# One order list of a fused attention and dense-layer kernel, rearranged; the last outputs finished one at a time

## The chip, the cores and the metric

The kernel runs on one core of a Trainium2 chip. The metric is the device time of one execution in microseconds; where several runs are shown, it is their median. The engines are called by the profile's names: PE multiplies matrices, DVE works on vectors, ACT applies functions, POOL does further element work, and SP issues most of the transfers.

## The reference

The input x has 2048 rows of 512 elements in bf16. It is normalized row by row (xn), and three terms are added: x itself, an attention with a compressed memory, and a dense layer with a gate function.

```python
xn = layernorm(x)
out = x + A(xn) + silu(xn @ w1) @ w2          # w1: 512 x 1792, w2: 1792 x 512

def A(xn):                                     # 32 heads of 16, 4 segments of 512 rows
    q, k, v = heads(xn @ wq), heads(xn @ wk), heads(xn @ wv)
    M, z = 0, 0
    for s in range(4):
        p = softmax(q[s] @ k[s].T * 0.25 + mask)            # each row sees itself and earlier ones
        a_mem = (phi(q[s]) @ M) / (phi(q[s]) @ z + 1e-6)    # phi(t) = t + 1 above 0, else exp(t)
        o[s] = g * a_mem + (1 - g) * p @ v[s]               # g = sigmoid(beta)
        M += phi(k[s]).T @ v[s];  z += sum(phi(k[s]))
    return o @ wo
```

## The kernel before

The work is cut into small pieces. Each piece is a word in one long string, `ORDER`, and the loop at the end of the kernel calls the pieces in exactly this order. Every engine gets its instructions in the order of the words and works through them in that order; what one engine needs of another is a wait. So the string fixes the queue of every engine, SP's transfers too. A word has a kind, then numbers: the segment s (0 to 3) first, then a block dt of 128 channels (8 heads), a row tile j of 128 rows or a block of w1's columns, then a part.

The score pieces `S0` to `S79` are the backbone. Each forms scores of eight heads' worth of queries and keys in the one four-bank PSUM tile psS, then issues the exponential on ACT (line 669) into one of seven buffers Pb, and the mask of the diagonal on POOL (line 677). Piece t belongs to segment t // 20, block (t // 5) % 4 and batch t % 5; batches 2, 3 and 4 also read kTo, a masked copy of the keys which POOL makes. In what follows a stage is what stands from one S to the next, numbered in the order of the list: stage 1 begins with S1. Each line of `ORDER` is one stage.

The other words:

- `k`, `q`, `v`, `h`: parts of the products of xn with wk, wq, wv, w1. `kv`, `qv`, `vv` copy a finished product out of PSUM on DVE, `ka`, `qa`, `va` on ACT; `kv` and `ka` also issue POOL's kTo. `ha` is the tanh on ACT and `hv` the product on DVE that makes hT.
- `E`, `O`: weighing, the product of Pb and v for even and odd heads (16 column-tiled matrix products, line 696). `Ev`, `Ov` copy the result on DVE, `Ea`, `Oa` on ACT; the even ones also issue two transfers on SP (the softmax sums to zraw), the odd ones six.
- `fp`, `fa`, `fv` and `gp`, `ga`, `gv`: phi of k and of q, on POOL, ACT and DVE. `t`: a transposing transfer of phi(k). `m`, `mv`, `mw`: the update of the memory.
- `s`, `sv`, `r`, `w`, and for the last segment `fill`, `R`, `W`: denominators and their reciprocals on DVE. `z`, `d`: two transfers each on SP that spread the reciprocals over the channels (spr). `zv`, `dv`: the products with them on DVE. `n`: the product phi(q) M, added to the attention output oT by `nv` on DVE.
- `o`, `oc`, `od`: one product of an output tile, whole, in halves or in quarters of its columns; products 0 to 13 read hT and w2, 14 to 17 read oT and wo. `oh` is the same for the very last tile (segment 3, row tile 3), which is done in two halves of 256 columns. `xl` loads 128 rows of x for the sum (x_res, line 579). `st` adds it and stores a whole tile of 128 x 512 (lines 586 and 591); `sh` does that for a half of the last tile (lines 633 and 637).
- `xs`, `xg`, `Nv`, `XD`, `X`, `Xv`, `Xa`: statistics, root, normalization and transposition of x. `X` transposes on PE, and `Xv` (DVE) or `Xa` (ACT) copies the result; `XD` is a transposing transfer. `lw` loads w2 and wo.

The tile psS takes four PSUM banks, and a pool of four more serves all other products; a piece that opens a product waits until the copy or addition that reads the bank's former content has ended. Tiles of x_res and of the normalized rows share four places in SBUF in the same way.

PE works in three tilings: rows (scores), columns (weighing, denominators) and whole. The k, q, v, h, m, n and o pieces can run whole (128 x 128) or as four column pieces of 32 (line 324); the loop picks, for the pieces after a score piece, the tiling of the next weighing piece or score piece that follows, so that few changes are needed.

Of the kernel before, what the change touches and what calls it, by code (L numbers as in the profile page):

```python
# [16 lines left out]
kind odd ones0 ones1 zeros xc0 xd0 xc1 xq0 xi0 Nv0 busy44 xd1 xq1 xc2 xi1 X0.1 Nv1 xd2 Xa0.1 busy6 v0.0.0 v0.0.1 xq2 X1.1 Xa1.1 xs3 v0.0.2 v0.0.3 xq3 v0.1.0 xi2 v0.1.1 v0.1.2 v0.1.3 Nv2 xi3 X2.1 va0.0 k0.2.0 va0.1 Nv3 Xv2.1 X3.1 Xv3.1 k0.0.0 k0.0.1 k0.0.2 k0.0.3 q0.0.0 kv0.0 tb q0.0.1 q0.0.2 xs4 q0.0.3 qa0.0 k0.2.1 q0.3.0 fa0.0 q0.1.0  # L17
S1 k0.2.2 xs6 q0.1.1 v0.3.0 v0.3.1 xs7 q0.3.1 q0.1.2 q0.1.3 xs5 xg4.4 q0.3.2 qa0.1 q0.3.3 fp0.0
S2 k0.2.3 v0.3.2 qv0.3 v0.3.3 k0.1.0 kv0.2 fp0.2 fa0.2 k0.1.1 vv0.3 k0.1.2 k0.1.3 q0.2.0 q0.2.1
S3 kv0.1 q0.2.2 h0.10.0 h0.10.1 Nv4 fv0.0 q0.2.3 h0.10.2 v0.2.0 h0.10.3 qv0.2 ha0.10 k0.3.0 k0.3.1  # L20
S0 Nv5 v0.2.1 k0.3.2 hv0.10 h0.11.0 k0.3.3 h0.11.1 h0.11.2 kv0.3 h0.11.3 Nv7 xs8 XD5 ha0.11 h0.7.0
S7 h0.7.1 h0.1.0 h0.7.2 h0.7.3 v0.2.2 h0.1.1 v0.2.3 XD4 h0.1.2 h0.1.3 hv0.11 Nv6 ha0.7
S6 h0.13.0 fp0.3 XD7 h0.13.1 vv0.2 hv0.7 E0 XD6 v1.1.0 h0.13.2 h0.13.3 ha0.1 v1.1.1 Ev0
S5 fv0.2 h0.5.0 v1.1.2 h0.5.1 hv0.1 v1.1.3 vv1.1 v1.3.0 h0.5.2 ha0.13 xs14 hv0.13 h0.5.3 ha0.5 t0.2 v1.3.1
S9 hv0.5 xs12 q1.1.0 v1.3.2 v1.3.3 fa0.3 q1.1.1 q1.1.2 E1 k1.1.0 q1.1.3
S4 qv1.1 k1.1.1 vv1.3 fv0.3 k1.0.0 k1.0.1 k1.0.2 lw0 h0.4.0 k1.1.2 Ev1 h0.4.1 k1.0.3 k1.1.3 kv1.1
S17 h0.8.0 h0.8.1 kv1.0 h0.4.2 O0 xs10 h0.4.3 h0.2.0 Ov0 ha0.4
S10 h0.2.1 k1.2.0 xs11 xs9 k1.2.1 h0.2.2 k1.2.2 h0.2.3 h0.8.2 ha0.2 t0.3 hv0.4 xg8.4 t0.0 k1.2.3
# [805 lines left out]
```

## Time and profile before

| | us |
|---|---|
| median of 3 runs | 228.55 (228.10 to 229.02) |
| the profiled execution | 229.09 |
| its span | 227.40 |
| PE, ACT, DVE, POOL busy | 217.2, 198.0, 177.7, 113.9 |
| S1 begins on PE | 12.27 |
| S78, the last score piece, begins | 206.18 |
| PE's last product ends | 223.60 |

The granted clock of PE is 1.00 throughout. The profile's times count from the start of the span. A line of the timeline has the start, the length, the engine with the line of the kernel, what is written from what, the number of instructions merged into it, and in square brackets how long the engine had been idle and what ended that. Lines with SPq are SP issuing transfers, not the transfers.

### The profile page before, as it was taken

To read this page: it belongs to the slowest core of one execution; us is meant where nothing else is said; L and a number is where in the kernel's file an instruction comes from. 1 tells how busy PE (TensorE), PEld (TensorE's weight loads), DVE (VectorE), ACT (ScalarE), POOL (GpSimd) and SP (SyncE) were. 2 spreads that over 40 slices of the span, in tenths; PEclk is the share of its full clock that TensorE was granted. 3 is DMA by queue.
4 is the path that set the end of the run, shared out by engine and by line. 5 is a ranking of instruction groups with operands and counts; after the bars stand their busy time and mean duration, and the time that the engine had idled before them with its cause. 6 is when DMAs were issued, how large, how long until landed. Compare 5 with 4: busy or idle time off the path is not lost.

```text
span 227.4 us, 7543 instructions
## 1 busy us (share of the span) xinstructions
PE 217.2 (96%) x3124; PEld 112.9 (50%) x3152; DVE 177.7 (78%) x351; ACT 198.0 (87%) x179; POOL 113.9 (50%) x173
## 2 busy tenths in 40 slices
PE   8999999999999999999999999999999999999993
PEld 8666645545534434444444434445444444445662
DVE  5799899987787897658798798747676888887834
ACT  3799998999999999999999899999999989897000
POOL 6059647667454673665644577546474265342000
PEclk9999999999999999999999999999999999999999
DMA  6992429323215213404314212141032212024122
GB/s 181 361 381 68 77 52 299 60 55 57 61 22 158 72 35 47 96 15 112 41 40 113 75 53 58 35 117 42 22 100 66 88 36 84 29 63 130 29 90 94
DMA packets 34787, 20.55 MB, mean 90 GB/s; under 512 B 15680, under 2 KB 34240, under 8 KB 34752
## 3 DMA queue, kind: packets, MB, share of 16 engines
q1 hardware_dynamic: 32128, 17.45, 28.3%
q10 hardware_dynamic: 2624, 2.62, 3.6%
q8 instruction: 24, 0.39, 0.8%
q14 instruction: 11, 0.09, 0.1%
HBM read 9.96 MB, written 2.10 MB: 53 GB/s over the span
## 4 chain that ended last, share of the span: by engine, by line
PE 62%; ACT 11%; DVE 11%; DMA 8%; issue 4%; SPq 2%; POOL 0%; DVEq 0%
PE ps L322 18%; PE psO L322 14%; PE psS L662 9%; ACT Pb L669 8%; PE ps L324 8%; PE psO L324 6%; PE psV L696 6%; DMA x_hi<-in_A_x_dram 4%; DMA spr<-rz 3%; ACT th L457 2%; DMA x_res<-in_A_x_dram 2%; DVE stats L272 1%; DVE o_out L586 1%; DVE kT L361 1%; PE psM L324 1%
## 5 line engine op out<-in xcount | busy, mean ns | idle before, releaser
L669 ACT ACTIVATE Pb<-psS 128x2048 bf16<-128x2048 f32 x80 | 150.2, 1878 | 5.8 <-PE psS L662 5.1
L677 POOL TENSOR_SCALAR_AFFINE_SELECT Pb<-Pb 128x512 bf16<-128x512 bf16 (+1 forms) x112 | 80.1, 729 | 85.1 <-ACT Pb L669 83.7
L462 DVE SCALAR_TENSOR_TENSOR hT<-th,ps 128x512 bf16<-128x512 bf16 x56 | 37.8, 679 | 14.1 <-ACT th L457 13.7
L322 PE MATMUL ps<-xnT,w_sb 128*128 128x512 bf16 (+1 forms) x177 | 43.3, 340 | 0.8 <-issue 0.5
L322 PE MATMUL psO<-w_sb,hT 128*128 128x512 bf16 (+2 forms) x139 | 36.1, 340 | 0.7 <-issue 0.5
L457 ACT ACTIVATE th<-ps 128x512 bf16<-128x512 f32 x56 | 32.8, 597 | 0.5 <-PE ps L322 0.4
L324 PE MATMUL psO<-w_sb,hT 128*32 128x128 bf16 (+2 forms) x468 | 26.7, 300 | 0.0
L322 PEld LDWEIGHTS <-w_sb 128*128 128x128 bf16 x184 | 17.1, 98 | 16.3 <-issue 3.3
L696 PE MATMUL psV<-Pb,Vz 128*32 128x128 bf16 (+3 forms) x512 | 23.1, 300 | 0.4 <-DVE oT L573 0.2
L322 PEld LDWEIGHTS <-hT 128*128 128x128 bf16 x149 | 13.6, 97 | 16.9 <-issue 4.8
L324 PE MATMUL ps<-xnT,w_sb 128*32 128x512 bf16 (+1 forms) x384 | 21.8, 329 | 0.0
L324 PEld LDWEIGHTS <-hT 128*32 128x32 bf16 x636 | 15.7, 97 | 9.7 <-issue 1.7
L696 PEld LDWEIGHTS <-Vz 128*32 128x32 bf16 x512 | 13.0, 96 | 10.6 <-issue 1.4
L662 PE MATMUL psS<-qT,kT 16*128 16x128 bf16 (+3 forms) x256 | 17.3, 301 | 0.9 <-ACT Pb L669 0.8
L662 PE MATMUL psS<-qT,kTo 32*128 32x384 bf16 (+3 forms) x256 | 17.2, 299 | 0.6 <-ACT Pb L669 0.2
L362 POOL TENSOR_SCALAR kTo<-kT,pm_odd 128x512 bf16<-128x512 bf16 x16 | 11.9, 747 | 8.2 <-DVE kT L361 7.3
L322 PE MATMUL ps<-xnT,wk_sb 128*128 128x512 bf16 (+1 forms) x66 | 15.4, 328 | 0.7 <-issue 0.5
L322 PE MATMUL ps<-wv_sb,xnT 128*128 128x512 bf16 x48 | 14.3, 380 | 0.6 <-issue 0.2
L662 PEld LDWEIGHTS <-kT 16*128 16x128 bf16 x256 | 5.9, 91 | 16.7 <-issue 16.2
L361 DVE CAST kT<-ps 128x512 bf16<-128x512 f32 x15 | 10.2, 687 | 4.6 <-PE ps L322 4.3
L586 DVE SCALAR_TENSOR_TENSOR o_out<-psO,x_res 128x512 bf16<-128x512 f32 x14 | 9.6, 687 | 5.3 <-PE psO L322 2.8
L719 DVE CAST oraw<-psV 128x512 bf16<-128x512 f32 x16 | 11.0, 688 | 3.4 <-PE psV L696 3.3
(105 smaller groups left out, 298.3 us busy)
## 6 DMA issues: line engine op xcount, KB each, us to landing
spr<-rz SPq DMA_DIRECT2D x56, 64.0 KB
x_res<-in_A_x_dram SPq DMA_DIRECT2D x16, 128.0 KB
out_dram<-o_out SPq DMA_DIRECT2D x15, 128.0 KB
w_sb<-in_B_w_dram SPq DMA_DIRECT2D x1, 1792.0 KB
w_sb<-in_B_w_dram ACTq DMA_DIRECT2D x1, 1792.0 KB
x_hi<-in_A_x_dram SPq DMA_DIRECT2D x2, 512.0 KB
oraw<-odd SPq DMA_DIRECT2D x64, 16.0 KB
wv_sb<-in_A_wv_dram SPq DMA_DIRECT2D x2, 256.0 KB
```

Of the source, the lines that this page charges most:

```text
L322: return [nc.tensor.matmul(out, lhsT=lhsT, rhs=rhs, start=start, stop=stop, skip_group_check=True)]
L324: nc.tensor.matmul(out[c : c + 32], lhsT=lhsT[:, c : c + 32], rhs=rhs, start=start, stop=stop, tile_position=(0, c), skip_group_check=True,)
L361: copy(out=kT[:, dt, :], in_=sts[s].pop(("k", dt))[:, :])
L362: nc.gpsimd.tensor_scalar(out=kTo[:, dt, :], in0=kT[:, dt, :], scalar1=pm_odd[:, 0:1], scalar2=1.0, op0=ALU.mult, op1=ALU.mult,)
L457: nc.scalar.activation(out=th[:], in_=sts[s]["h", ft][:, :], func=AF.Tanh, scale=0.5)
L462: nc.vector.scalar_tensor_tensor(out=st["hT"][:, ft, :], in0=st.pop(("th", ft))[:], scalar=1.0, in1=st.pop(("h", ft))[:, :], op0=ALU.add, ...
L586: out = nc.vector.scalar_tensor_tensor(out=o_out[:], in0=st.pop(("psO", j)), scalar=0.5, in1=st["x", j][:], op0=ALU.mult, op1=ALU.add)
L662: nc.tensor.matmul(psS[:, g, c0 : c0 + nq], lhsT=kk[rows, dt, kt * P : (kt + 1) * P], rhs=st["qT"][rows, dt, kt * P : L], start=True, stop ...
L669: exp = nc.scalar.activation(out=Pb[:, :, :], in_=psS[:, :, :], func=AF.Exp, scale=SCALE)
L677: mask = nc.gpsimd.affine_select(out=blocks, in_=blocks, compare_op=ALU.is_ge, fill=0.0, base=0, pattern=[[0, blocks.shape[1]], [1, P]], c ...
L696: nc.tensor.matmul(psV[32 * g : 32 * g + 32, kt * P : L], lhsT=Vzs[s % 2][:, kt, 4 * dt + g, par : par + 2, :].rearrange("p a d -> p (a d) ...
L719: copy(out=oraw[:], in_=sts[s].pop(("psV", 0))[:, :])
```

## The change

Only the string `ORDER` differs. It has 1324 words before and after, and all but six are the same words at other places. Six change the engine of a copy: `Xv2.1` becomes `Xa2.1`, `kv3.2` becomes `ka3.2` and `ka3.3` becomes `kv3.3`, `Ov14` becomes `Oa14`, `Ev15` becomes `Ea15`, and `Oa15` becomes `Ov15`. The order of the score pieces changes too, near where they stood (the first are S1 S2 S3 S0 S7 S6 S5 before and S1 S4 S2 S5 S0 S3 S7 after). The last outputs end in the order st3.0, sh0, st3.2, st3.1, sh1 before, and sh1, st3.2, st3.0, sh0, st3.1 after, with other products between them; two of the residual loads stand before them in the last stage, xl3.1 and xl3.0 before, xl3.1 and xl3.2 after.

The diff, cut to the stages that the prediction speaks of (each line one stage; the last is the whole last stage):

```diff
-kind odd ones0 ones1 zeros xc0 xd0 xc1 xq0 xi0 Nv0 busy44 xd1 xq1 xc2 xi1 X0.1 Nv1 xd2 Xa0.1 busy6 v0.0.0 v0.0.1 xq2 X1.1 Xa1.1 xs3 v0.0.2 v0.0.3 xq3 v0.1.0 xi2 v0.1.1 v0.1.2 v0.1.3 Nv2 xi3 X2.1 va0.0 k0.2.0 va0.1 Nv3 Xv2.1 X3.1 Xv3.1 k0.0.0 k0.0.1 k0.0.2 k0.0.3 q0.0.0 kv0.0 tb q0.0.1 q0.0.2 xs4 q0.0.3 qa0.0 k0.2.1 q0.3.0 fa0.0 q0.1.0
-S1 k0.2.2 xs6 q0.1.1 v0.3.0 v0.3.1 xs7 q0.3.1 q0.1.2 q0.1.3 xs5 xg4.4 q0.3.2 qa0.1 q0.3.3 fp0.0
...
-S3 kv0.1 q0.2.2 h0.10.0 h0.10.1 Nv4 fv0.0 q0.2.3 h0.10.2 v0.2.0 h0.10.3 qv0.2 ha0.10 k0.3.0 k0.3.1
...
-S7 h0.7.1 h0.1.0 h0.7.2 h0.7.3 v0.2.2 h0.1.1 v0.2.3 XD4 h0.1.2 h0.1.3 hv0.11 Nv6 ha0.7
...
-S5 fv0.2 h0.5.0 v1.1.2 h0.5.1 hv0.1 v1.1.3 vv1.1 v1.3.0 h0.5.2 ha0.13 xs14 hv0.13 h0.5.3 ha0.5 t0.2 v1.3.1
-S9 hv0.5 xs12 q1.1.0 v1.3.2 v1.3.3 fa0.3 q1.1.1 q1.1.2 E1 k1.1.0 q1.1.3
...
-S49 ga2.3 kv3.2 dv1.1 o1.0.13 k3.0.0 Ev9 Ov8 gv2.2 o1.2.1 k3.0.1 n1.2 kv3.0 o1.2.7 zv1.1 o1.0.11 nv1.2
-S51 o1.2.2 h2.0.0 o1.2.8 h2.0.1 gp2.0 o1.0.6 n1.1 ha2.0 o1.2.16
-S54 o1.2.11 mw1.0 zv1.3 o1.2.12 od1.2.5.3 nv1.1 z1.0 o1.2.6 o1.0.10 hv2.0 xl2.3 gp2.3 O9 oc1.2.10.1 oc1.0.9.0 Ov9 od1.2.5.2 n1.3 ga2.0
...
-S53 o1.0.17 od1.2.5.1 oc1.1.9.1 od1.1.7.2 gv2.3 o1.0.8 mw1.2 E10 o1.2.17 o1.2.14 o1.1.11 oc1.1.9.0 ga3.3 Ev10
...
-S78 o3.0.5 h3.11.0 o2.1.17 st2.1 h3.11.1 E15 o3.0.6 o3.2.1 oh1.1 o3.1.8 Ev15 ha3.11 oc3.0.3.1 oh0.1 O15 oh12.1 o3.2.3 o3.2.5 hv3.11 zv3.1 oh5.1 o3.2.8 n3.2 Oa15 oh13.0 o3.1.3 o3.1.12 dv3.1 zv3.2 nv3.2 o3.2.7 oc3.0.11.1 oc3.0.11.0 oh9.0 n3.0 oh16.0 n3.1 zv3.0 o3.2.9 o3.1.1 oc3.1.0.1 o3.1.13 o3.2.0 oc3.1.0.0 o3.2.12 o3.2.6 nv3.0 od3.1.11.2 nv3.1 oh11.1 o3.1.14 oh15.1 o3.2.11 oh0.0 R1.1 R1.0 oh10.0 o3.0.14 od3.0.10.2 oh8.0 od3.1.11.3 d3.3 oh15.0 od3.0.10.0 R1.3 o3.1.6 R1.2 oc3.1.9.0 oc3.1.9.1 o3.1.5 oh2.0 o3.1.10 W1 oh14.0 o3.2.13 oh1.0 o3.1.15 oh5.0 o3.0.15 o3.0.16 dv3.3 z3.3 od3.0.10.1 o3.2.15 xl3.1 o3.2.16 zv3.3 o3.2.2 n3.3 oh11.0 od3.1.11.1 oh3.1 oh10.1 oh6.0 oh4.1 nv3.3 o3.1.4 od3.0.10.3 oh4.0 oh12.0 o3.2.4 o3.0.13 oc3.0.3.0 oh3.0 o3.0.17 xl3.0 st3.0 o3.2.14 od3.1.11.0 oh7.0 o3.2.17 oh17.0 oh7.1 sh0 o3.2.10 o3.1.2 oh2.1 o3.1.7 o3.1.16 st3.2 o3.1.17 oh17.1 st3.1 oh6.1 oh13.1 oh14.1 oh16.1 oh8.1 oh9.1 sh1
+kind odd ones0 ones1 zeros xc0 xd0 xc1 xq0 xi0 Nv0 busy44 xd1 xq1 xc2 xi1 X0.1 Nv1 xd2 Xa0.1 busy6 v0.0.0 v0.0.1 xq2 X1.1 Xa1.1 xs3 v0.0.2 v0.0.3 xq3 va0.0 v0.1.0 v0.1.1 xi2 Nv2 xi3 v0.1.2 Nv3 v0.1.3 X2.1 va0.1 k0.0.0 X3.1 k0.0.1 k0.2.0 Xv3.1 k0.2.1 Xa2.1 k0.0.2 k0.0.3 q0.0.0 q0.0.1 q0.0.2 tb q0.0.3 q0.1.0 kv0.0 k0.2.2 xs5 qa0.0 q0.3.0 fa0.0
+S1 k0.2.3 k0.1.0 xs6 kv0.2 q0.1.1 xs4 q0.1.2 q0.1.3 xs7 k0.1.1 k0.1.2 qa0.1 q0.3.1 fp0.0 xg4.4 k0.1.3 kv0.1
...
+S3 XD6 XD7 v1.1.0 xs10 hv0.7 h0.5.2 h0.5.3 ha0.5 h0.1.3 xs12 v1.1.1 XD4 v1.1.2 v1.1.3 vv1.1 h0.13.0 h0.13.1 ha0.1 hv0.5
+S7 xl0.1 xs11 h0.13.2 h0.13.3 hv0.1 v1.3.0 v1.3.1 E0 ha0.13 v1.3.2 Ev0
...
+S50 o1.0.10 od1.2.5.0 n1.1 kv3.0 h2.0.0 h2.0.1 o1.2.9 nv1.1 o1.2.6 ha2.0 n1.3
+S51 oc1.2.0.0 nv1.3 hv2.0 t2.3 o1.2.16 o1.2.15 O9 o1.0.8 o1.1.8 Ov9 o1.2.4 zv1.0 o1.1.0
...
+S52 o1.2.11 ga3.3 o1.0.15 oc1.1.4.1 oc1.2.10.0 xl2.3 oc1.2.10.1 dv1.0 hv2.2 od1.2.5.3 od1.1.7.3 n1.0 od1.2.5.2 o1.2.17 oc1.2.0.1 od1.2.5.1 nv1.0 o1.1.3 o1.2.7
+S56 o1.0.14 o1.2.14 E10 gv2.3 o1.2.13 o1.2.2 oc1.1.9.0 fa2.2 o1.0.16 Ev10 o1.2.12
...
+S64 od1.3.12.0 r2.1 h2.9.1 hv2.10 r2.2 h3.1.0 w2 h3.1.1 d2.1 o2.3.0 gp3.2 z2.3 oc1.3.1.0 od1.3.12.1 o2.3.6 ha2.9 ha3.1 st1.3 hv2.9 o2.3.7
+S60 hv3.1 oc2.3.13.0 fill o2.3.3 h3.3.0 h3.3.1 m2.2 d2.3 h3.0.0 ha3.3 od2.3.9.0 mv2.2
...
+S66 h2.12.1 h3.4.0 h3.4.1 o2.0.1 ha2.12 od2.3.9.3 oc2.3.2.1 ha3.4 o2.0.8 o2.0.4
...
+S78 hv3.11 o3.1.12 dv3.1 o3.1.5 z3.0 o3.1.2 o2.1.15 z3.2 E15 o3.0.12 o3.0.8 o2.1.6 dv3.2 o3.2.12 oh11.1 o3.0.1 oh9.1 z3.1 oh1.1 Ea15 O15 oh7.1 o3.0.7 o3.1.1 Ov15 d3.3 oc3.1.9.1 o3.0.5 o3.2.0 n3.2 od3.0.10.3 oh2.0 od3.1.11.0 zv3.2 od3.0.10.2 zv3.0 od3.0.10.1 oh6.1 od3.1.11.1 oh13.1 o3.1.4 o3.1.13 nv3.2 oh10.1 od3.0.10.0 n3.0 od2.1.12.0 o3.2.9 oh5.1 o3.2.2 nv3.0 od3.1.11.3 R1.3 oh8.1 oc3.0.3.1 oh16.0 o3.2.14 R1.0 o3.1.14 o3.2.1 R1.1 oh14.0 oc3.0.3.0 o3.1.3 R1.2 oh4.1 W1 zv3.1 oh3.1 oc3.0.11.1 oh9.0 n3.1 oh7.0 z3.3 oh8.0 o3.0.14 oh5.0 o3.2.8 o3.2.6 oh13.0 xl3.1 oh10.0 st2.1 o3.2.4 o3.2.5 nv3.1 o3.2.3 o3.0.16 dv3.3 oc3.1.9.0 oh14.1 o3.2.16 o3.0.15 oh6.0 zv3.3 oh16.1 o3.2.13 oh15.1 o3.0.13 xl3.2 n3.3 nv3.3 o3.2.10 o3.2.15 o3.2.7 o3.2.11 oh2.1 od3.1.11.2 oh12.1 oh0.1 oh17.1 o3.0.17 oc3.0.11.0 o3.2.17 oh4.0 o3.1.15 oh0.0 o3.1.7 sh1 oh1.0 o3.1.10 st3.2 oh15.0 oc3.1.0.0 oh11.0 st3.0 oh12.0 oh3.0 oh17.0 o3.1.17 o3.1.16 sh0 o3.1.8 oc3.1.0.1 st3.1
```

## The prediction

> **What bounds the kernel now.** I read the page's busy shares first, then busy times by stretch, then the order of time around single stages and at the end. The change is one list of pieces in another order, so what counts is where an engine waits.
>
> ```profile
> PE 217.2 (96%) x3124; PEld 112.9 (50%) x3152; DVE 177.7 (78%) x351; ACT 198.0 (87%) x179; POOL 113.9 (50%) x173
> L669 ACT ACTIVATE Pb<-psS 128x2048 bf16<-128x2048 f32 x80 | 150.2, 1878 | 5.8 <-PE psS L662 5.1
> ...
> 12.27:36.86 24.59, 23.38 (x324) 14.77 (x328) 23.36 (x47) 23.58 (x21) 15.53 (x22) 1.00 0.51 153
> 36.86:61.00 24.14, 23.29 (x359) 12.60 (x363) 20.58 (x43) 24.06 (x22) 16.00 (x24) 1.00 0.38 89
> 206.18:223.60 17.42, 17.42 (x441) 11.04 (x440) 11.61 (x23) 2.95 (x3) 0.85 (x2) 1.00 0.25 74
> 223.60:227.40 3.80, 0.00 (x1) 0.00 (x0) 0.69 (x2) 0.00 (x0) 0.00 (x0) 1.00 0.36 116
> ```
>
> The last four rows are stretches of the span: length, then busy PE, PEld, DVE, ACT, POOL. PE and ACT are both full to the 80th score piece at 206.18, then PE alone is, to 223.6; 3.8 us follow without PE. In the first stretch (ten stages) DVE is 95% busy too.
>
> ```profile
> 65.82 0.39 PE L662 MATMUL psS<-qT,kTo 32*128 32x512 bf16 x4
> 66.27 1.88 ACT L669 ACTIVATE Pb<-psS 128x2048 bf16<-128x2048 f32 x1
> 68.20 0.39 PE L662 MATMUL psS<-qT,kT 16*128 16x512 bf16 x4
> 68.64 1.88 ACT L669 ACTIVATE Pb<-psS 128x2048 bf16<-128x2048 f32 x1 [0.50 <-PE psS L662]
> ```
>
> This is the ring that sets the pace: a score piece, 0.45 us later its exponential of 1.88, 0.05 later the next score piece, since the one psS tile must be free: 2.38 us from S to S. One tanh (0.60) on ACT takes the 0.50 that is idle here. On PE a 512-column product costs 0.216 start to start, a weighing piece 0.54, a score piece 0.335. A stage whose PE work sums to 2.28 also lasts 2.38, so each stage costs max(2.38, PE work + 0.105).
>
> **The part that is arithmetic.** Both lists have the same number of score, weighing and product pieces (202.06 us of PE work by these prices) and, as the code picks the tiling, 160 changes of tiling each. By the rule the 79 stages from S1 to S78 sum to 192.46 us before and 192.40 after (PE work in them 180.55 and 180.49; work a stage lacks to 2.28: 3.62 and 3.61): -0.06. Measured before: 206.18 - 12.27 = 193.91. So only 1.45 us are waits in the stages, and these the change can gain or lose.
>
> **The waits of before, and what becomes of them.**
>
> ```profile
> 22.25 0.10 PEld L662 LDWEIGHTS <-kTo 32*128 32x128 bf16 x4 [0.29 <-POOL kTo L362]
> 29.14 1.08 ACT L457 ACTIVATE th<-ps 128x512 bf16<-128x512 f32 x2
> 30.09 1.90 ACT L669 ACTIVATE Pb<-psS 128x2048 bf16<-128x2048 f32 x1
> 136.49 0.45 PEld L696 LDWEIGHTS <-Vz 128*32 128x32 bf16 x16 [0.72 <-DVE oT L573]
> ```
>
> Fifth stage (S7), 0.29: kT's copy kv0.1 comes two stages before its use. The new list has it in stage 1 and S7 in stage 7: -0.29.
>
> Eighth stage (S9), 0.25: two tanh pieces in one stage start the next exponential at 30.09, 0.35 later than 29.29 + 0.45. The new list has a pair in S3, and the next stage (S7) has only 1.96 us of PE work, so all 0.37 shows: +0.12. The pair of S16 (0.25 over two stages) has its twin in the new S15: 0. New pairs stand in S64 and S66; the next stages hold 2.44 and 2.55 us of PE work, which cover 0.16 and 0.27 of 0.37 each: +0.30. Before, the late pairs stood beside a stage of 2.93 us and cost nothing.
>
> Stage 52 (S54), 0.43: weighing piece O9 waits for a PSUM bank that nv1.1 frees late; DVE had 5.31 us of work put into stage 50 (two kv at 0.69, Ev, Ov and nv at 0.69, gv 0.83, zv 0.56, dv 0.47). The new list puts at most 2.6 us into any of stages 48 to 52, but O9 still follows the adder of its bank (nv1.3) by only 0.43 us of PE work. Bounds -0.43 and 0; I take -0.43, as DVE no longer runs late. Stage 55, 0.22: E10 waits for a mask. There S52's mask (1.1 us) now precedes E10 at 0.87 us of PE work: stays.
>
> **What the change adds early.** Stages 1 to 10 gain one more statistics pair (0.67 + 0.18) and one more hT (0.66) on DVE: 23.36 + 1.51 = 24.87 us for 24.59. What is late on DVE frees banks late, and the h and k products wait for these. Bounds: 0 (PE works on what it has) and +1.5 (all of it shows); I take the overload, +0.30, as DVE's 1.2 us of idle time there can be filled. In stages 11 to 20 DVE has 2.4 us less, so the debt ends there.
>
> **Head.** X2.1's copy moves from DVE (0.42) to ACT (a 512-wide copy there, 0.59, row of Vz), behind va0.1 which ends at 9.57: k0.0.2 may start at 10.2 for 10.08: S1 +0.07. The exponential's table load behind it ends at 11.6, before qa0.0's input.
>
> **The end.** Times from S78 = 0 (206.18).
>
> ```profile
> 218.06 0.43 SPq L579 DMA_DIRECT2D x_res<-in_A_x_dram  x1
> ...
> 221.75 0.69 DVE L586 SCALAR_TENSOR_TENSOR o_out<-psO,x_res 128x512 bf16<-128x512 f32 x1 [1.52 <-PE psS L324]
> 222.35 0.41 DVE L633 SCALAR_TENSOR_TENSOR o_half<-psS,x_res 128x256 bf16<-128x256 f32 x1
> ...
> 223.28 0.68 DVE L586 SCALAR_TENSOR_TENSOR o_out<-psO,x_res 128x512 bf16<-128x512 f32 x1
> ...
> 223.88 0.41 DVE L633 SCALAR_TENSOR_TENSOR o_half<-psS,x_res 128x256 bf16<-128x256 f32 x1
> 224.77 0.34 SPq L637 DMA_DIRECT2D out_dram<-o_half  x1
> ```
>
> Before, the first output addition starts when the load issued at 218.06 has landed (its bracket names PE, but the chain that ended last names this load, 3.60), and five additions run back to back: 0.60 after a whole one, 0.34 after a half one. DVE ends at 18.11, the last store goes out at 18.59, the span ends at 21.22.
>
> After, PE has 17.03 us of work for 17.19 and ends at 17.26. Counting products back, sh1 has its last product 1.73 before that, st3.2 1.40, st3.0 1.08, sh0 0.32, st3.1 at the end. sh1 can start at 15.73 (0.2 from product to reader), then DVE again sets the spacing: 16.07, 16.67, 17.27, 17.61, end 18.30: +0.19. So the outputs are spread in the list but not on DVE. The final store was issued 0.48 after DVE's end; the other four 0.03 to 0.15. I take 0.25: -0.23. The final store is 128 KB for 64 KB, which took 2.63 from issue to the span's end; a 128 KB load took 3.60. Bounds 0 and +0.97; +0.20, nearer the row that is a store. The end: +0.16.
>
> [...]
>
> SP's queue is in order: the list now puts xl3.2, one of the four residual loads, behind O15's six moves (to 8.3), d3.3 (to 9.5), z3.3 (must wait for W1: nv3.0 ends at 7.4, four reciprocals 1.80, W1 0.35, so 9.6 to 10.9), xl3.1 (11.4) and st2.1's store (11.85). It lands at 11.9 + 3.60 = 15.5; st3.2 needs it at 16.07: hidden, by 0.57. xl3.0 moves out of this queue to stage 76. Ea15 for Ev15 and Ov15 for Oa15 trade 0.59 on ACT for 0.69 on DVE: O15's moves start 0.1 later, covered by the same 0.57.
>
> **Sum.** 0.07 - 0.06 - 0.29 + 0.12 + 0.30 - 0.43 + 0.30 + 0.16 = +0.17 us. The profiled execution (229.09, of it span 227.40) becomes 229.26, span 227.57. It lies 0.54 above the median of the runs, 228.55, which becomes 228.7.
>
> **Rivals.**
>
> *DVE sets the pace early (slower).* The early overload isn't absorbed: every stage from the second to the tenth waits for banks, the whole 1.5 us shows: 228.7 + 1.2 = 229.9. For: 95% busy there already, and the additions come in the first eight stages. Against: DVE waited 1.2 us there, and stages 7, 12 and 16 of the new list have PE work of 1.96, 1.85 and 1.42, room to catch up. It decides once more than some 0.5 us of PE waits on DVE fall into stages 2 to 10. Chance 0.16.
>
> [...]
>
> *The late residual load (slower).* If W1 comes over 0.57 late, st2.1's store and xl3.2 slip with it, and st3.2, st3.0, sh0, st3.1 wait on DVE behind it. A slip of 1.5 costs 0.9: 229.6; with other lost waits over 229.7. For: the load chain ended last before. Against: two fewer DMAs stand ahead of the z's. Chance 0.10.
>
> *The waits go and none come (faster).* All 1.45 us vanish, -0.06, and the end gains 0.3: 226.7. Half of it is enough for a clear gain. For: DVE's peaks fall from 5.31 to 4.2 us a stage. Against: tanh pairs and E10. Chance 0.18.
>
> **Numbers.** No measurable change: 0.56. A measurement tells some 0.5% (1.14 us) from no change. Slower by more: 0.16 + 0.10 = 0.26; faster by more: 0.18. The likeliest case's own range is 227.6 to 229.6. The range for 8 in 10 takes in the dear end of the first rival and a little of the last: 227.4 to 230.2.
>
> **What would show it.** Right: S from 12.3 to about 206.2 in steps of 2.38; no wait for kTo in S7 and none for nv1.1 at O9; a late exponential after S3, S64, S66; five additions at the end 0.34 and 0.60 apart; x_res never the last to arrive. Wrong: PE waits on DVE before 37 us over 0.5 in sum; DVE waiting on xl3.2's landing; a stage with a wait over 0.5 that this list doesn't name.

## The result, and the profile after

The change makes the kernel slower: the median of 22 runs is 231.52 us (229.89 to 234.27), for 228.50 before (22 runs, 227.87 to 230.96); the ratio is 1.0123, 95% interval 1.0104 to 1.0142. The forecast was 228.7 with a range up to 230.2. Ratios, here and below, leave out runs more than 1.5% above the fastest of their kernel; medians are of all runs. The profiled execution took 232.43 (before: 229.09), with a span of 230.8 (227.4).

The busy shares, the clock row and the exponential's group of the page after:

```profile
PE 222.0 (96%) x3026; PEld 113.6 (49%) x3026; DVE 173.4 (75%) x349; ACT 199.0 (86%) x181; POOL 112.5 (49%) x173
...
PEclk9999999999799999999999999999999999999999
...
L669 ACT ACTIVATE Pb<-psS 128x2048 bf16<-128x2048 f32 x80 | 150.2, 1878 | 7.2 <-PE psS L662 5.9
```

Busy time by stretch after, from S1 on (length; PE, PEld, DVE, ACT, POOL busy; PE's granted clock; DMA share; GB/s):

```profile
12.47:36.86 24.39, 23.43 (x276) 14.13 (x277) 23.59 (x48) 22.99 (x20) 15.12 (x22) 1.00 0.53 144
36.86:61.00 24.14, 21.85 (x320) 11.50 (x321) 17.25 (x34) 21.50 (x21) 13.67 (x21) 0.93 0.46 97
209.60:227.34 17.74, 17.44 (x441) 11.05 (x440) 11.31 (x23) 2.57 (x3) 1.71 (x3) 1.00 0.23 70
```

The busy shares don't show the loss; PE is even busier, at 222.0. The second stretch does: PE, ACT and DVE all work less there (21.85, 21.50, 17.25 us) than before (23.29, 24.06, 20.58), and the granted clock is 0.93 where it was 1.00. S78 begins at 209.60 for 206.18; the end behind it takes 21.20 for 21.22.

To place the loss I took the start of each score piece from the timeline, subtracted what the prediction's rule gives for the stage (the larger of 2.38 and its PE work + 0.105), and summed the excess:

| | before | after |
|---|---|---|
| S1 begins | 12.27 | 12.47 |
| rule, 79 stages | 192.46 | 192.40 |
| excess, stages 1 to 10 | 0.65 | 1.19 |
| excess, stages 11 to 20 | 0.21 | 3.13 |
| excess, stages 21 to 79 | 0.59 | 0.41 |
| S78 to the end of the span | 21.22 | 21.20 |
| span | 227.40 | 230.80 |

Stages 11 to 20 hold 2.92 of the 3.40 us that the span grew, nearly all of it in stage 18 (S15): 5.30 us for 2.50 by the rule. The next fence is the timeline around it (SPq rows are SP issuing):

```profile
53.89 1.21 SPq L413 DMA_TRANSPOSE phiK<-pk  x1
...
54.53 0.41 PE L324 MATMUL psM<-Vz,phiK 128*32 128x128 bf16 x16
...
56.35 0.41 PE L324 MATMUL psM<-Vz,phiK 128*32 128x128 bf16 x16 [1.42 <-DMA phiK<-pk]
...
57.42 1.29 PE L696 MATMUL psV<-Pb,Vz 128*32 128x512 bf16 x16
```

PE does the first half of m0.0, then stands 1.42 us until t0.1's transposing transfer has landed, which SP issued only at 53.89. In the list of before it was issued at 49.44, and m0.0 ran both halves from 54.27 on without a wait:

```profile
54.27 0.62 PE L324 MATMUL psM<-Vz,phiK 128*32 128x128 bf16 x32
```

After the change, behind the pause the work itself is slow: a weighing piece takes 1.29 us, elsewhere 0.72. Busy time by stretches of 1 us shows why:

```profile
56.00:57.00 1.00, 0.65 (x28) 0.56 (x32) 0.19 (x1) 0.52 (x1) 0.35 (x1) 1.00 0.60 123
57.00:58.00 1.00, 1.00 (x20) 0.62 (x16) 0.31 (x2) 0.31 (x1) 0.90 (x2) 0.52 0.43 83
...
60.00:61.00 1.00, 1.00 (x29) 0.71 (x28) 0.64 (x2) 0.84 (x1) 0.00 (x0) 0.77 0.01 4
```

The third number from the end is PE's granted clock. It falls to half 0.7 us after PE works again: 0.52 means full speed until 57.04, 0.77 half speed until 60.46, and the two slices between have 0.50. The trace's own record of the clock has 3.413 us at half, so 1.71 us of work are lost. Not every execution has it: of the 22 runs, nine show a mean clock of 0.990 to 0.993, their median 232.43, and 13 show 0.997 to 1.000, their median 230.71.

Why SP was late is seen in its own waits from 30 to 60 us (us in total, times, longest) and in its queue after the change; the last fence is its queue before:

```profile
SPq L711 <- DMA w_sb<-in_B_w_dram: 2.4, 1, 2.4
```

```profile
39.31 3.49 SPq L711 DMA_DIRECT2D zraw<-oraw  x2
...
45.48 1.97 SPq L749 DMA_TRANSPOSE xnT<-xn_t  x1
...
52.52 1.26 SPq L749 DMA_TRANSPOSE xnT<-xn_t  x1
```

```profile
48.13 1.21 SPq L749 DMA_TRANSPOSE xnT<-xn_t  x1
49.44 1.21 SPq L413 DMA_TRANSPOSE phiK<-pk  x1
```

Two things are new. First, XD8 (the row at 45.48) now stands ahead of t0.1, t0.2 is issued in this stretch too (before at 28.73), and O1's six moves come a stage later; from 47.51 on SP issues without a gap. Second, Ev1's second move of 2 KB, inside the row at 39.31, has nothing to do with w2 and yet waits 2.4 us for the 1.75 MB load of it. In both traces the 256 transfers of SP and ACT take eight completion semaphores in turn (the marks by which a reader knows that a transfer has landed). After the change lw0, issued at 33.01, has number 107; Ev1's second move, the eighth transfer behind it, has 107 again and is issued at 42.27, 0.02 us after the load's last mark on it (42.25).

### The profile page after: what moved, and what is told of

It reads as the page before. It is cut to its first block, busy times and chain, and to the rows that moved or that the text cites. A ratio compares the mean times of both kernels' runs of the same rounds, so it can differ in the third digit from the quotient of the medians.

```text
span 230.8 us, 7322 instructions
## 1 busy us (share of the span) xinstructions
PE 222.0 (96%) x3026; PEld 113.6 (49%) x3026; DVE 173.4 (75%) x349; ACT 199.0 (86%) x181; POOL 112.5 (49%) x173
## 4 chain that ended last, share of the span: by engine, by line
PE 62%; ACT 16%; DVE 8%; DMA 5%; issue 5%; POOL 1%; SPq 1%; DVEq 0%; POOLq 0%; ACTq 0%
PE ps L322 25%; ACT Pb L669 12%; PE psO L322 9%; PE psS L662 8%; PE psO L324 6%; PE psV L696 6%; PE ps L324 6%; ACT th L457 3%; DMA wv_sb<-in_A_wv_dram 2%; ACT ex L395 2%; DVE hT L462 1%; POOL Pb L677 1%; DVE xn_t L301 1%; DMA phiK<-pk 1%; DVE o_out L586 1%
## 5 line engine op out<-in xcount | busy, mean ns | idle before, releaser
L322 PE MATMUL ps<-xnT,w_sb 128*128 128x512 bf16 (+1 forms) x209 | 48.3, 338 | 0.5 <-DVE Vz L378 0.5
L324 PE MATMUL psO<-w_sb,hT 128*32 128x512 bf16 (+2 forms) x452 | 28.1, 316 | 0.0
L322 PEld LDWEIGHTS <-w_sb 128*128 128x128 bf16 x209 | 19.1, 98 | 17.2 <-issue 4.1
L696 PE MATMUL psV<-Pb,Vz 128*32 128x384 bf16 (+3 forms) x512 | 23.6, 305 | 0.2 <-POOL Pb L677 0.2
L662 PE MATMUL psS<-qT,kT 16*128 16x512 bf16 (+3 forms) x256 | 17.3, 301 | 0.9 <-ACT Pb L669 0.6
L324 PE MATMUL ps<-xnT,w_sb 128*32 128x512 bf16 (+1 forms) x284 | 17.8, 351 | 0.0
L662 PE MATMUL psS<-qT,kTo 32*128 32x128 bf16 (+3 forms) x256 | 17.4, 303 | 0.3 <-ACT Pb L669 0.3
L726 DVE CAST odd<-psV 128x512 bf16<-128x512 f32 x15 | 10.3, 687 | 8.3 <-PE psV L696 8.3
L322 PE MATMUL ps<-wv_sb,xnT 128*128 128x512 bf16 x55 | 16.0, 380 | 0.3 <-DMA wv_sb<-in_A_wv_dram 0.2
L322 PE MATMUL ps<-xnT,wq_sb 128*128 128x512 bf16 (+1 forms) x67 | 14.7, 329 | 0.0
```

Source lines behind the costliest of these rows:

```text
L322: return [nc.tensor.matmul(out, lhsT=lhsT, rhs=rhs, start=start, stop=stop, skip_group_check=True)]
L324: nc.tensor.matmul(out[c : c + 32], lhsT=lhsT[:, c : c + 32], rhs=rhs, start=start, stop=stop, tile_position=(0, c), skip_group_check=True,)
L662: nc.tensor.matmul(psS[:, g, c0 : c0 + nq], lhsT=kk[rows, dt, kt * P : (kt + 1) * P], rhs=st["qT"][rows, dt, kt * P : L], start=True, stop ...
L696: nc.tensor.matmul(psV[32 * g : 32 * g + 32, kt * P : L], lhsT=Vzs[s % 2][:, kt, 4 * dt + g, par : par + 2, :].rearrange("p a d -> p (a d) ...
L726: copy(out=odd[:], in_=sts[s].pop(("psV", 1))[:, :])
```

## The experiments

Words are moved in the list of before or after; a diff shows only what moved. Stage numbers stay.

**The transfer earlier.** `e1_t01_early`:

```diff
-S12 ... h1.11.3 XD11 xs15 ...      S14 ... qv1.3 t0.1 h0.0.3 ...
+S12 ... h1.11.3 t0.1 XD11 xs15 ... S14 ... qv1.3 h0.0.3 ...
```

> The changed list with one piece moved: t0.1, the transposing transfer of phiK that m0.0 reads, stands ahead of XD11 on SP's queue instead of behind it (one transfer of 1.26 us earlier). Late transfer (theory): it is issued at about 52.6 us for 53.9 and lands near 55.0 for 56.35, PE's wait of 1.42 us at m0.0 shrinks to 0.1, and with the pause the clock of 0.5 goes too: stage 18 lasts 2.5 to 2.6 us for 5.30, and the median falls from 231.5 to about 228.8. Early DVE overload (rival): the loss lies in stages 2 to 10, stage 18 is only where a debt shows, m0.0 waits for something else: within 0.3 of 231.5. Clock by chance (rival: the half clock has nothing to do with the pause): the pause's 1.4 us go, the clock's 1.5 us stay in part of the runs: 230.1, with granted clocks of 0.993 still among the runs.

Ratio 1.0077 (1.0046 to 1.0107); the profile's stage 18 exceeds the rule by 0.16 for 2.81. But the median of all runs is 232.81, where 228.8 was expected: six of twelve runs took 233.8 to 234.6, five of them at 0.990 to 0.993. The profile, of one of the other six, tells part of it: the queue is as long as before, so the next in it is late. Stage 20 now exceeds the rule by 0.74, PE waiting 0.68 us for XD10's transfer (k2.2.0 reads it). The place was right, the cure too small. What halves the clock in five runs, with the pause at m0.0 gone, isn't shown.

**The hold away.** `e2_lw0_later`:

```diff
-S8 ... O0 lw0 kv1.0 ...   S16 ... Ev1 fp0.1 ...
+S8 ... O0 kv1.0 ...       S16 ... Ev1 lw0 fp0.1 ...
```

> The changed list with the load of w2 (lw0) moved behind Ev1: every piece that SP issues keeps its place, but the semaphore of the eight that DMAs use in turn which the load takes is now next used by a move of Ov1, not by Ev1's second move. Late transfer by the shared semaphore (theory): SP no longer stands 2.4 us at 39.8, everything behind it on the queue comes up to 2.4 us earlier, t0.1 lands by 55, and pause and half clock go: about 228.8. Rival that SP is simply full with DMA issues of 1.2 us each (the order of the list, not the semaphore): the hold goes but t0.1 is still issued after 53 us and m0.0 still waits over 1 us: over 230.5. Rival DVE: 231.5.

Median 230.29, ratio 1.0064 (1.0038 to 1.0090). The hold is gone, t0.1 is issued at 52.80, m0.0 waits 0.19 us for 1.42, stage 18 exceeds the rule by 0.40 and stage 20 by nothing. The profiled span, 230.1, is nevertheless long, for another reason (below, the late gather).

**The reader later.** `e3_m00_later`: m0.0 from S15 to behind Ev3 in S19, mv0.0 to the end of S18.

> The changed list with the reader moved instead of the transfer: m0.0 behind Ev3 in the next stage (S19), mv0.0 at the end of S18. Late transfer: PE has other work until 58 us, the transfer lands at 56.35 as before and nobody waits: stage 18 (S15) lasts about 2.4, S19 takes the 0.45 us of m0.0's work and gets longer by 0.2 to 0.45; the half clock goes; 228.8 to 229.2. Rival DVE or clock by chance: 230 to 231.5, with granted clocks of 0.993 in part of the runs.

Missed: 230.99, ratio 1.0122 (1.0077 to 1.0166). Stage 18 is clean and no run of the six has a clock below 0.997, so in these runs the half clock is gone with the pause. But stages 19 and 20 exceed the rule by 0.48 and 0.94: XD9 and XD10 are issued 54.62 to 58.2, and m0.0 now stands where the work was already full. It is the queue, not one transfer.

**The same fault made in the list of before.** `e4_before_pause` moves t0.1 behind Ev2, `e11_before_long_pause` one transfer further, behind XD8.

> The list of before with one piece moved, to make the same fault there: t0.1 from S11 to behind Ev2, some 4 us later on SP's queue; it is issued near 54.4 for 49.4 and lands near 56.9, while m0.0 stands at 54.27. Late transfer with the clock: PE stands 2 to 2.6 us at m0.0, then the granted clock falls to 0.5 for some 3 us in a large part of the runs: 228.5 + 2.4 = 230.9 without, 232.5 with the clock; granted clocks of 0.99 among the runs. Pause without the clock: 230.9 in all runs at clock 1.00. Rival DVE: the transfer has room, below 229.3.

> The list of before with t0.1 one transfer later still than in the run with the pause of 1.18 us (behind XD8 instead of behind Ev2). The pause at m0.0 becomes 2.2 to 2.6 us, on the list of before. Clock by the length of the pause (theory): where 1.18 us never brought the half clock in 12 runs and 1.42 did in about 10 of 22, this does in most runs: 228.5 + 2.4 = 230.9 without and about 232.5 with, the latter in more than half of the runs, clock 0.993. Rival, the clock hangs on something in the changed list: all runs near 230.9 at 1.0.

e4: PE waits 0.91 us in the profile, where 2 to 2.6 were expected; 229.50, ratio 1.0033 (1.0010 to 1.0057), no clock below 0.998 in twelve runs. e11: PE waits 2.29 us; 232.13, ratio 1.0159 (1.0133 to 1.0184), three of four runs at 0.992 or 0.993. Its pause, and its clock by the microsecond:

```profile
57.25 0.41 PE L324 MATMUL psM<-Vz,phiK 128*32 128x128 bf16 x16 [2.29 <-DMA phiK<-pk]
```

```profile
58.00:59.00 1.00, 1.00 (x20) 0.54 (x16) 0.20 (x2) 0.60 (x1) 0.00 (x0) 0.62 0.43 107
61.00:62.00 1.00, 1.00 (x28) 0.66 (x24) 0.12 (x2) 0.91 (x1) 0.03 (x1) 0.67 0.08 21
```

Half clock from 58.24 to 61.66: 3.41 us again, and 1 us after the pause. One moved word gives the list of before the time of the changed one.

**Work in the pause.** `e10_filled_pause`, on the changed list:

```diff
         for i in range(2):
             dt = d0 + i
+            for _ in range(24 if (s, d0, i) == (0, 0, 1) else 0):
+                product(psM[:, 1, :], wk_sb[:, 0, 0:P], wk_sb[:, 0, 0:P], True, True)
             for j in range(TPS):
```

> The changed list with 24 products of 128 columns added on PE (1.30 us by 0.054 each) in front of the second half of m0.0: they write the part of the PSUM tile that the real products then start afresh, so they fill the pause of 1.42 us with work that nobody needs. Clock falls because PE stands (theory): the transfer is as late as before, stage 18 keeps 1.4 to 1.6 us of excess, but no run has the half clock there: granted clocks of 0.997 to 1.0 only, all runs between 229.9 and 231.8. Rival, clock falls for another reason (power, chance): a third of the runs are still at 0.993 and 232.2 or more. If the transfer lands early in some runs, these are up to 1.3 us longer for the filler.

All six runs at 0.998 to 1.000, where nine of 22 without the filler were below 0.994: by chance this happens in some 4% of cases ((13/22)^6). The time did not gain, 232.48 for at most 231.8 expected: the filler takes its 1.3 us also where the pause is shorter, and in the profile PE stands again for 0.93 us, in the weighing piece that follows, with no releaser shown.

**Both moves of the early queue.** `e9_sp_both` is e1 and e2 together; `e14_sp_both_look` one more execution of it.

> The changed list with both moves of SP's early queue: lw0 behind Ev1 (no hold of 2.4 us on the semaphore of the w2 load) and t0.1 ahead of XD11. Early SP queue (theory): t0.1 and the last two of XD8 to XD11 are issued 2 us earlier, neither m0.0 (stage 18) nor k2.2.0 (stage 20) waits: stages 11 to 20 exceed the rule by 0.2 to 0.3 us for 3.13, no half clock; the profile's S78 at 206.6 to 207.0, the runs from 227.3 (end of 21.2) to 229.5 (end with the late gather, up to 23.5), median below 230.3 of the one move and 232.8 of the other. Rival, SP has nothing to do with it and the single moves only shifted the phase of something else: stages 11 to 20 keep 0.8 us or more, and runs above 232 at a clock of 0.993 stay.

> The list with both moves of the early queue, one execution more. If it is one of the long ones (232.6 or more, a third of them): late gather at the end (theory): S78 at 206.4 as before, PE stands 2 us or more for z3.3's spreading, the granted clock falls to 0.5 within 2 us of it, the end is 24 to 26 us. Rival, a stall earlier: S78 at 209 or later, the end 21.2. If it is one of the short ones: S78 near 206.4 and an end of 21.2, and nothing is told apart.

Stages 11 to 20 exceed the rule by 0.27 (3.13 in the changed list, 0.21 before), S78 begins at 206.38; e14 gives 0.27 and 206.48. The ratio falls from 1.0123 to 1.0043 (1.0027 to 1.0059), the median is 229.60. But four of the twelve runs took 232.6 to 233.9 at 0.990 to 0.993, and e14 was a short one.

**The end.** In four of eleven profiles with the changed end it takes longer: 23.0 us (e2), 23.6 (e3), 24.4 (e12) and 22.4 (e6), in the other seven 20.9 to 21.5. In the first three DVE waits 2.6 to 3.2 us for the last gather, z3.3's spreading of rz (0.95 in e9); in e6 that wait is 0.95, and it is mainly the last store that lands late, 3.4 us after its issue for 2.7. With the end of before, all eight profiles lie between 20.97 and 21.9. `e12_end_moved` is e9 with st2.1 and xl3.2 behind zv3.3, `e13_both_old_end` is e9 with the order of before behind its 75th stage.

> The changed list with both moves of the early queue (as e9) and st2.1 and xl3.2 moved behind zv3.3, so that the store of st2.1 and the residual load behind it are not on the DMA engines while z3.3's spreading of rz is. Late gather by sharing with store and load (theory): the end is 21.2 us in every run, the runs spread less than those of e9 and their median is 0.5 to 1.0 lower. Rival, the gather is late by itself: the same as e9, with ends of 22.4 to 23.5 in the profile. Rival, xl3.2 becomes the last to land: the end is 21.5 to 22 in all runs, DVE waits for it at st3.2.

> The changed list with both moves of the early queue for its first 75 stages, and the order of before for what is left (the last four stages and the end). The join puts some 0.5 us more PE work into the stages and less behind them. A third of the runs with both moves took 232.6 us or more at clocks of 0.990 to 0.993, though stages 11 to 20 wait no longer. Late gather at the end plus a half clock behind PE's wait for it (theory): these runs are gone, all runs lie between 228.7 and 230.5 at 0.997 to 1.0, the end is 21.0 to 21.3 us in the profile. Rival, something earlier in the changed order stalls PE in a third of the runs: a third of these runs too lie above 232 at 0.993.

e12 is worse: 231.60, ratio 1.0140 (1.0089 to 1.0190), end 24.4. The store was away and the gather was late all the same, so the theory of sharing with the store falls. First the wait in e9, then in e12, then e12's packets over the stretch 219.99 to 221.79 just ahead of its landing:

```profile
219.62 0.42 DVE L554 TENSOR_TENSOR oT<-spr,oraw 128x512 bf16<-128x512 bf16 x1 [0.95 <-DMA spr<-rz]
```

```profile
221.82 0.42 DVE L554 TENSOR_TENSOR oT<-spr,oraw 128x512 bf16<-128x512 bf16 x1 [3.21 <-DMA spr<-rz]
```

```profile
q1 hardware_dynamic: 26, 0.02, 5.2%
```

In that stretch 26 packets keep 5.2% of 16 DMA engines busy, about the work of one. The trace lists them one by one: 16 packets of 512 B, as the gather moves them, then eight of 1 KB (the residual load behind it) and two of 4 B. z3.3's second transfer has 128 packets of 512 B; 112 start within 1.7 us of its issue, as all 128 do in e9, and 16 come in a row afterwards. In e12 the first of the 16 starts at 220.28, just as a packet of code (16 KB, on a queue that the profile calls instruction, 218.65 to 220.30) ends; in e2 it is 220.66 for code until 220.67, in e3 222.12 for code until 222.13. So in all three late gathers one eighth of the transfer starts within 0.02 us of the end of a packet of code, as if it had stood behind it. That both were on one engine is my reading and not shown: the trace doesn't name the engine of a packet. Nor can it be the whole of it: in e16 below code starts at the same distance behind the issue as in e12, 1.27 us, and holds nothing (DVE waits 0.96 us).

e13: 230.21, ratio 1.0054 (1.0027 to 1.0081), no run above 231.15 and none below 0.999; the join costs 0.26 by the rule and 0.4 in stage 76. The long runs of e9 are gone with its end. That would fit a half clock behind the late gather, but other runs speak against it: e16 keeps the changed end and has none of these runs either, and in the three profiles with a late gather PE stands 2.19, 2.34 and 2.79 us for it without a fall of the clock while PE still has work. In e12, for example, the stretch after the pause is at 1.00 (third number from the end):

```profile
223.50 0.29 PE L324 MATMUL psS<-wo_sb,oT 128*32 128x256 bf16 x4 [2.79 <-DVE oT L573]
```

```profile
222.48:225.89 3.41, 2.38 (x68) 1.81 (x72) 1.55 (x4) 0.00 (x0) 0.00 (x0) 1.00 0.26 79
```

What the long runs of e9 are stays open; no profile caught one.

**Parts of the one list joined to parts of the other.** `e5_early_after`: 18 stages of after, then the order of before. `e6_early_before`: the reverse. `e7_tail_after`: 75 stages of before, then after. `e8_mid_after`: before to 18, after to 75, before.

> The first 18 stages (head to S15, some 59 us) from the changed list, the rest in the order of before; only xl0.1 and fp1.2 of the early part keep their old places. Early SP queue (theory): the whole loss sits here. Stages 1 to 10 last 0.55 us longer than before (DVE, stage 5 above all), m0.0 waits 1 to 1.5 us for phiK in stage 18, in part of the runs the clock falls to 0.5 behind it: median 230.3 to 231.5, best runs near 229.8. The end is that of before: from S78 to the span's end 21.2. Rival, late gather at the end: the loss over before is 0.55 plus at most 0.5, median 229.3.

> The first 18 stages from the list of before, the rest in the changed order. Early SP queue: no wait for phiK, no half clock, stages 1 to 20 as before; what remains is the middle (0 to 0.4 less) and the end: 228.3 to 228.8. Late gather at the end (rival, or second cause): in part of the runs the last spreading of rz (z3.3) lands 1.5 to 2 us later, behind a store and two residual loads that are issued within 1 us of it, and PE stands 2.2 us for it: runs from 228.2 to 230.5, median 229.3.

> The list of before for 75 stages and only the last four stages and the end (outputs completed one by one, spread out) in the changed order. The end as predicted: +0.16 us, 228.7, all runs alike. Late gather at the end (rival): runs spread from 228.3 to 230.5, in the profile either PE's longest gap after S78 is 0.3 us and the end 21.2 long, or DVE waits 2.6 us for spr<-rz, PE 2.2, and the end is 23 long.

> First 18 stages of before, stages 19 to 75 in the changed order, the end of before. Both theories: neither the early waits nor the late gather, so the middle alone: the wait for O9's bank (0.43) and the mask's (0.22) change by -0.4 to +0.1, 228.0 to 228.6, clock 1.00 in every run. Rival, the middle costs too (waits that the profiled runs don't show): over 229.

Medians 233.20, 231.19, 229.72, 230.70; ratios 1.0199 (1.0159 to 1.0239), 1.0101 (1.0065 to 1.0137), 1.0028 (0.9999 to 1.0056), 1.0090 (1.0063 to 1.0117). As totals they are inconclusive: the joins cost up to 0.7 us by the rule (e7: 193.16) and make waits of their own (e5 1.78 us in stage 20, e6 0.76 there, e8 0.40 in stage 76). By stage they agree with the table: early order of after, 1.19 in stages 1 to 10 and two of six runs at 0.993, though m0.0 waits only 0.43 us in the profile (e5); early order of before, 0.62 to 0.69 and no run below 0.995; stages 21 to 40 within 0.1 of the rule in all four. e7 puts the changed end, gather in time, at 21.0; its profile also has 1.01 us of wait at O9, of which more below.

**The early DVE order.** `e16_both_mended` is e9 with:

```diff
-S5 q0.2.1 h0.11.0 v0.3.3 Nv4 q0.2.2 h0.11.1 Nv6 q0.2.3 vv0.3 h0.11.2 qv0.2 h0.11.3 ha0.11 hv0.10
+S5 q0.2.1 h0.11.0 v0.3.3 q0.2.2 h0.11.1 q0.2.3 vv0.3 h0.11.2 qv0.2 Nv4 h0.11.3 ha0.11 hv0.10 Nv6
-S56 o1.0.14 o1.2.14 E10 gv2.3 o1.2.13 o1.2.2 ...
+S56 o1.0.14 o1.2.14 gv2.3 o1.2.13 o1.2.2 E10 ...
```

> The changed list with both moves of the early queue, and Nv4 and Nv6 (each 0.6 us of DVE) moved behind the copies vv0.3 and qv0.2 in S5, E10 behind three products in S56. Early DVE order (theory for stage 5): the stage S0 waited 0.45 us for Vz's copy, which stood behind two xn_t on DVE; with the copy ahead of them its excess falls from 0.64 to 0.2 or less, E10's 0.35 to 0.1: the short runs fall by 0.6 to 228.4, with S78 near 205.7. Rival, DVE is simply full there (95% busy before): the excess moves to the next stages, stages 1 to 10 keep 1.1 to 1.2 us.

Stage 5 had been long because vv0.3's copy stood behind two xn_t on DVE, seen here in the changed list:

```profile
20.43 1.81 DVE L301 TENSOR_SCALAR xn_t<-x_hi,mv_all,rstd_all 128x512 bf16<-128x512 bf16 x2
22.16 0.67 DVE L378 CAST Vz<-ps 128x512 bf16<-128x512 f32 x1
22.89 2.23 PE L322 MATMUL ps<-xnT,w_sb 128*128 128x256 bf16 x18 [0.45 <-DVE Vz L378]
```

Stages 1 to 10 fall from 1.19 to 0.68 (before: 0.65), stages 41 to 60 from 0.45 to 0.11, S78 begins at 205.57, and the median is 228.78, ratio 1.0000 (0.9975 to 1.0024), all twelve runs at 0.999 or 1.000. Five moved words give back all that the change lost.

**The waits of before mended.** `e15_before_mended` and, without the move of the tanh, `e17_before_two`:

```diff
-S5 ... h0.5.3 ha0.5 t0.2 v1.3.1
-S9 hv0.5 xs12 q1.1.0 v1.3.2 v1.3.3 fa0.3 q1.1.1 ...
+S5 ... h0.5.3 t0.2 v1.3.1                                 # e15 only; fa0.3 into S4, fv0.3 into S17
+S9 ha0.5 xs12 q1.1.0 v1.3.2 v1.3.3 hv0.5 q1.1.1 ...       # e15 only
-S54 ... gp2.3 O9 oc1.2.10.1 oc1.0.9.0 Ov9 od1.2.5.2 n1.3 ga2.0
+S54 ... gp2.3 oc1.2.10.1 oc1.0.9.0 od1.2.5.2 O9 Ov9 n1.3 ga2.0
-S53 ... mw1.2 E10 o1.2.17 o1.2.14 ...
+S53 ... mw1.2 o1.2.17 o1.2.14 E10 ...
```

> The list of before with three of its own waits mended: ha0.5 into S9 (hv0.5 some PE pieces later, fa0.3 into S4, fv0.3 into S17), so that no stage has two tanh (0.25 in S9); O9 and Ov9 behind three small output products (0.27 us of PE work later; the wait there was 0, 0.43 and 1.02 us in three profiles of this order); E10 behind two output products (0.43 us later; the mask's wait was 0.22). Theory of the stage rule (a stage lasts the larger of 2.38 us and its PE work + 0.105, the rest are waits): 0.25 + 0.27 + 0.22 = 0.7 us less at most, the stage sum 193.2 to 193.5 for 193.9, median 227.7 to 228.2. Rival, the waits come back one stage later: 228.4 and more.

> The list of before with only the two small late moves: O9 and Ov9 behind three small output products (0.27 us of PE work), E10 behind two (0.43 us). Stage rule: of the two waits 0.43 and 0.22 go at least 0.27 and 0.22, stages 41 to 60 exceed the rule by 0.2 us or less for 0.61, median 0.3 to 0.6 us lower than before. Rival, the wait for O9's bank hangs on when a spreading of rz lands (0, 0.43 and 1.02 us in three profiles), so it comes and goes with the execution and the moves don't show in the median: within 0.2 us of before.

e15 is slower, 231.53, ratio 1.0119 (1.0076 to 1.0163). Its stage 8 shows part of why:

```profile
31.22 0.59 ACT L457 ACTIVATE th<-ps 128x512 bf16<-128x512 f32 x1
31.85 0.69 DVE L462 SCALAR_TENSOR_TENSOR hT<-th,ps 128x512 bf16<-128x512 bf16 x1 [0.87 <-ACT th L457]
32.59 0.40 PE L324 MATMUL ps<-xnT,wk_sb 128*32 128x512 bf16 x4 [1.45 <-DVE hT L462]
```

Behind the exponential the tanh ends 2.81 us after its score piece (at 29.00) for 0.93 before, its PSUM bank stays taken about as long, and PE waits 1.45 us for it: the pair of tanh that I took for a fault of 0.25 us was cheap. Later, in stage 20, PE stands another 1.45 us, for XD10's transfer; that wait wasn't followed up. e17: 228.50, ratio 1.0003 (0.9988 to 1.0019). Its profile has only 0.18 of excess in stages 41 to 60, but so has an untouched order in other executions (e4, e5 and e11: 0.0). The rival was right: those waits belong to the execution. No version here beats the kernel before.

## Why the prediction was wrong

The step that failed is the assumption under the sum: that of the early stages only DVE's load and kT's copy had to be checked. **SP's queue** was followed for the last stage alone (xl3.2, hidden by 0.57), not for t0.1 and m0.0, although the list moves lw0, Ev1, Ov1, XD8, XD11, t0.2 and t0.1 against each other. A followed queue would have shown XD8's and t0.2's issues ahead of t0.1 and O1's moves a stage later; that puts t0.1 some 3.4 us later (e2, without the hold: 52.80 for 49.44), against an estimated slack of about 2.5: it lands 2.46 us after its issue (53.89 to 56.35), before therefore near 51.9, for a reader at 54.5. The hold on the shared semaphore adds the other 1.1 us (53.89 for 52.80) and decides the size of the wait, 1.42 us for 0.19 in e2; no wait in the profile of before shows such a hold. The prediction's own sign of error, a stage with a wait over 0.5 that its list doesn't name, is stage 18. The **clock** was not a term at all: 1.7 us in nine of 22 runs. The first rival, DVE early, had the direction of the miss and part of its place (0.54 us), not its mechanism.

Term by term:

- Rule and PE work: -0.06 forecast; every profile of the whole changed list fits the rule to 0.1 us in stages 21 to 40.
- Head, +0.07: S1 began between 11.99 and 12.59 in profiles with the changed head; can't be told.
- S7's wait for kTo, -0.29: gone. The pair of S3, +0.12: S7 exceeds the rule by 0.36 where a pair before cost 0.26; right.
- Pairs of S64 and S66, +0.30: mis-sized, 0. The exponentials behind them start 0.58 and 0.63 after their score piece for 0.45, only 0.13 and 0.18 late, because the stages of the pairs themselves last 2.60 and 2.54 us; PE work covers that.
- O9, -0.43: gone, but it was no property of the order. In three profiles of the order of before this wait was 0.43, 1.02 (e7) and 0 (e4), with the landing of a spreading of rz that zv1.1 on DVE waits for: 0.27, 0.77 and 0 us. I put it down to DVE's load; that was the cause named wrong. First before, then e7:

```profile
135.20 0.64 DVE L554 TENSOR_TENSOR oT<-spr,oraw 128x512 bf16<-128x512 bf16 x1 [0.27 <-DMA spr<-rz]
```

```profile
135.68 0.72 DVE L554 TENSOR_TENSOR oT<-spr,oraw 128x512 bf16<-128x512 bf16 x1 [0.77 <-DMA spr<-rz]
```

- E10's mask, 0.22: 0.34. `e16_both_mended` moved E10 and took it away.
- Early DVE, +0.30 between 0 and 1.5: stages 1 to 10 lost 0.54 net, of which the order in S5 made 0.5 (e16). The rival (1.2 us, every stage waits) did not happen; 0.45 us of PE waits on DVE was what the trace shows there, just short of its point of decision.
- The end, +0.16: 21.20 for 21.22 in the profiled execution. The five additions came 0.35, 0.59, 0.60 and 0.42 apart, as reckoned, DVE 18.49 after S78 for 18.30. The last store went out 0.03 behind DVE (0.25 taken), and its 128 KB took 2.68 to the span's end, 0.05 more than the 64 KB before (0.20 taken). So the total was near because errors of 0.19, 0.22 and 0.15 partly cancel. The same holds for xl3.2: it went out 13.72 after S78, not 11.9, and was there all the same when st3.2 began, at 16.19, so it took at most 2.5 us and not 3.60; that was luck. In other executions the end is 1.2 to 3.2 us longer. That rival was named by the wrong transfer: in three of the four it is the gather z3.3 that is late, not xl3.2, which DVE never waited for in the profile after.

## What to carry to other kernels

When an order written by hand or by a search is changed, follow each in-order queue through every stage where it moves, the one that issues transfers first: its issues cost time one after the other (here some 0.6 us for a move, 1.2 for a transposing transfer), and one of them that waits (here 2.4 us, for a load that merely shares its completion semaphore) delays all behind it. A pause of PE can have two prices, its length and what the clock does afterwards; here a pause of 1.42 us cost up to 1.7 more. And a wait seen in one profiled execution is a property of the order only if other executions show it; before it is counted as a gain, look at what releases it.

## What the runs showed of the hardware

- PE's granted clock can fall to half after a pause of PE of 1.4 us. After the change the trace's clock record has full clock for 51.20 us, half for 3.413 us from 57.04 on, then full clock for 170.67 us; before, full clock for 221.87 us, to 4.0 us behind PE's last product. The full stretches are 15, 50 and 65 times the 3.413. In e11 the half clock lasts 3.41 us too, from 58.24 to 61.66. It began 0.7 and 1 us after PE had resumed; after the change PE was busy for 1.78 of the 3.42 us ahead of the fall, and for all of the 3.41 us at half.
- The pause's length alone doesn't decide. The mean clock was 0.990 to 0.993 in none of twelve runs where the profiled pause was 0.91 us (e4), in nine of 22 where it was 1.42, in three of four where it was 2.29 (e11). But in single profiles the clock held after 1.45 us twice (e15; mean clock of the execution 0.996), 2.19 (e2, 0.997), 2.34 (e3, 0.999) and 2.79 (e12, 0.997); after the change and in e11 it was 0.993. What decides stays open.
- A transfer of 2 KB waited 2.4 us for an unrelated one of 1.75 MB through a shared completion semaphore.
- The reader of a 64 KB gather issued in the same place waited 0.92 to 0.96 us in e1, e6, e9, e14 and e16, and 2.6 to 3.2 in e2, e3 and e12. In these three, 112 of its 128 packets came in time and 16 started within 0.02 us of the end of a 16 KB packet of code; in e16 such a packet passed and held nothing.
